# Graph tensor product on one Trainium2 core: the bf16 pieces of the edge features and a seventh one-hot row made by ScalarE

## The chip, the cores and the metric

The kernel runs on one core of a Trainium2 chip. The core has engines that run side by side, each through its own queue of instructions in a fixed order: TensorE (PE, matrix products; the profile shows its weight loads apart as PEld), VectorE (DVE, elementwise work), ScalarE (ACT, elementwise functions of one input), GpSimd (POOL, which issues the indirect transfers here) and SyncE (SP, which issues the plain ones). An engine that needs something from another waits for it, and what stands behind the waiting instruction in its queue waits too. The metric is the device time of one execution in microseconds. Lower is better.

## What is computed

```python
N, deg, C, L, DE = 10000, 64, 64, 1, 4
E = N * deg                                      # 640000 edges
M = (L + 1) ** 2                                 # 4
R = _silu(edge_feat @ w_rad)                     # (E, C)
xs = x[src]                                      # (E, C, M)
tp = jnp.einsum('eci,ef,ifo->eco', xs, Y, cg)    # (E, C, M)
msg = R[:, :, None] * tp
agg = _segment_sum(msg.reshape(-1, C * M), dst, N).reshape(N, C, M)
return jnp.einsum('ncm,cd->ndm', agg, w_mix)
```

Every edge fetches the 256 numbers of its source node, scales them by a small function of its four features, mixes them with its four numbers `Y`, and adds the result to its destination node. Source and destination are random.

## The kernel before

**Sorting.** The edges are cut into three parts (30, 35.5 and 34.5% of them). Each part is sorted by destination in two passes: `pass1` into 18 groups of 576 nodes, `pass2` of each group into up to 18 buckets of 32 nodes. A part and a group together are a segment. A pass works in chunks of 12 (first pass) or 11 (second) tiles of 128 edges. For a chunk, `spread` (lines 569 and 572, DVE) writes the edges' nine words into slots of rows (`X`), `rows` (lines 588 to 595) makes one one-hot matrix of 128 x 128 per tile (`oh`), which says to which row of the chunk an edge goes, `move` (lines 602 and 604, PE) multiplies the two, `evict` (line 609, ACT) copies the product out of PE's memory to `rt`, and `store` (line 613) has POOL scatter the rows to DRAM.

A one-hot is made in one of two ways. DVE compares (line 588): all its tiles in one instruction, 128 elements a tile. ACT squares the difference (line 594, one instruction of 128 elements per tile, into `sq`) and then takes relu(1 - 2 x square) of all its tiles in one (line 595). `ps.act`, 6 for both passes, is the number of tiles of a chunk that ACT does; DVE does the rest, so 6 of 12 or 5 of 11. Where a row of the chunk before is carried on, ACT squares one more (`tg`). `tables` computes where the rows of a pass go, in many small steps on all engines.

**Messages.** `messages` goes through units; a unit is one bucket of one part, with 5 tiles of 128 edges in the first part and 6 in the other two, 939 units in all. For a unit, `gather` (line 893, POOL) fetches the source rows with one indirect transfer per tile into one of seven buffers `xg`; `turn` (line 911, PE) turns the features, `turned` (line 916, ACT) copies them to `sT`, `radial` (lines 923 and 924, PE) multiplies with the weights, `silu` (line 927, ACT) applies the function; `spots` (lines 935 and 938, DVE) makes the destination one-hot times `Y`; `products` (line 945, DVE) scales `xg`; `sums` (line 958, PE) adds up the bucket; `evict` (lines 987 and 989) takes the sums out, and for the last part `mix` (line 1006) applies the output weights.

PE's `turn` is done in bf16 and the features are fp32, so each feature is split into three bf16 pieces that add up to it. `pieces` (lines 883 and 885, DVE) does this for a block of five buckets at once: cast the feature to bf16, written three times over (`e`); subtract the piece from the feature (`er`); cast the rest; subtract; cast. That is three casts and two subtractions a block, 210 blocks.

**Order.** In the first phase (up to some 500 us) only the first part is sorted. In the main phase the order of PE, DVE and ACT is the order in which the program text writes the instructions. `messages` is the outer loop: step k has four quarters, and in each quarter the listed functions are written for the unit k plus the given number (so `(silu, 1)` in step k is for unit k + 1). Between two quarters `groups` writes as many steps of the sorting of later parts and segments as are due. The order of POOL and SP is set by a scheduler from the dependences. `gather` stands five units ahead of `sums`.

Of the kernel before, what the change touches and what calls it, by code (L numbers as in the profile page):

```python
# [18 lines left out]
F = mybir.dt.float32  # L19
BF = mybir.dt.bfloat16  # L20
# [5 lines left out]
P = 128  # L26
B = 18
# [46 lines left out]
class Kernel:  # L74
# [276 lines left out]
    def tables(self, ps, D, nt, rows, kov, base, cap):  # L351
# [6 lines left out]
        assert N <= ps.NC <= 26 and nt >= T  # L358
        NC = ps.NC
        w = lambda nm, k, p=P, b=1, d=F: wk.tile([p, k], d, name=nm, tag=nm + ps.key, bufs=b)  # L360
# [12 lines left out]

        sums = w("sums", B * (T + 1))
        nc.vector.tensor_tensor_scan(sums[:H], ps.on, ps.cols, 0.0, op0=OP.mult, op1=OP.add)
# [39 lines left out]

        first, at = w("first", B), w("at", T * B)
        if ps.carry:
# [17 lines left out]
        eye = self.ident[:N, :N].unsqueeze(2).to_broadcast([N, N, J])  # L435
        bs, bd = w("bs", NC * J, NC, d=BF), w("bd", NC * J, NC)
        blk = lambda t: t[:N, :N * J].rearrange("p (c j) -> p c j", j=J)
# [74 lines left out]
    def route(self, ps, quad, nt, table):  # L512
# [65 lines left out]
        def rows(c):  # L578

            row, _ = MS[c // (2 * Q)]  # L580
            o = c % (2 * Q) * T
            m = min(T, nt - c * T)
            (_, _, _, tg), i = table(c)
            on = ps.carry and i > 0
            oh = self.ph.tile([P, 12, P], F, name="oh", bufs=3)
            v = max(m - ps.act, 0)
            if v:
                nc.vector.tensor_tensor(oh[:, :v, :], self.v128.unsqueeze(1).to_broadcast([P, v, P]),  # L588
                                        row[:, o:o + v].unsqueeze(2).to_broadcast([P, v, P]), op=OP.is_equal)

            at = [row[:, o + u:o + u + 1] for u in range(v, m)] + ([tg[:, i - 1:i]] if on else [])
            sq = self.ph.tile([P, 7, P], F, name="sq")
            for u, to in enumerate(at):
                nc.scalar.activation(sq[:, u, :], self.i128, AF.Square, bias=to, scale=-1.0)  # L594
            nc.scalar.activation(oh[:, v:v + len(at), :], sq[:, :len(at), :], AF.Relu, bias=self.ones[:, 0:1], scale=-2.0)  # L595
            XO[c] = (XO[c], oh, m, on)
# [235 lines left out]
    def messages(self):  # L832
# [4 lines left out]
        n = len(units)  # L837
        IDX, XG, PRE, ST_, RT, SS, VS, GP, GS, OLD, E9 = ({} for _ in range(11))

# [12 lines left out]
        def index(k):  # L852
# [16 lines left out]

        def pieces(k):  # L870

            g, j, s = units[k]
            if s or j % HB:
                return
            ut = sum(SPLIT[g[0]][1])
            a, z = j, min(j + HB, self.nb(g[1]))
            v = self.pay[g][:, a:z, :].rearrange("p b (t w) -> p (b t) w", w=W)[:, :, 5:9]
            n = (z - a) * ut
            E9[g, j // HB] = ph.tile([P, HB * MT, 3, 3, 4], BF, name="e9", bufs=2)
            r = ph.tile([P, HB * MT, 4], F, name="er", bufs=1)[:, :n]  # L880
            for q in range(3):
                e = E9[g, j // HB][:, :n, :, q, :]
                nc.vector.tensor_copy(e, (r if q else v).unsqueeze(2).to_broadcast([P, n, 3, 4]))
# [126 lines left out]
        def mixed(k, po):  # L1010
# [195 lines left out]
    def run(self):  # L1206
# [63 lines left out]
```

## Time and profile before

| | before |
|---|---|
| median of three runs | 8670.53 us (8667.58 to 8680.19) |
| span of the profiled execution, first to last instruction | 8660.7 us |
| what lies around the span, against the median | 9.8 us |
| busy: PE, DVE, POOL, ACT | 6942.9, 7173.7, 6041.3, 4089.0 us |
| gathers (line 893) | 5321 transfers, 5067.8 us of POOL |
| casts of `pieces` (line 883) | 630, of which 216 from 700 to 3300 us |

The profile has one execution. A row of a group of instructions gives its line, engine, operation, what it writes and reads, how often it ran, its busy time and the mean length of one, and behind a bar the idle time of the engine just before it and what ended that. A row of waits reads: engine, what waited, by what it was released, total us, how many times, the longest. The profiled execution's own time is not given apart from its span; the span is 6.9 us below the fastest of the three runs.

### The profile page before, as it was taken

What the parts mean: (1) busy time and instruction counts of PE and PEld (TensorE: products, weight loads), DVE (VectorE), ACT (ScalarE), POOL (GpSimd) and SP (SyncE); (2) the same over time, 40 slices, a digit from 0 to 9 for tenths busy, and PEclk for the clock granted to TensorE, in tenths of its full rate; (3) what the DMA queues carried; (4) which work ended last, traced back from release to release, by engine and by line L of the source; (5) the groups of instructions that cost most, each with busy time, mean ns of one, the idle gap of its engine ahead of it and who ended that gap; (6) DMA issues with size and microseconds to landing.
All of it is one profiled execution on the core that took longest, in us unless ns stands there. A gap on an engine that the chain in (4) does not pass through costs nothing. (4 is left out here: it accounts for less than half of the span.)

```text
span 8660.7 us, 149335 instructions
## 1 busy us (share of the span) xinstructions
PE 6942.9 (80%) x52148; PEld 6380.0 (74%) x52148; DVE 7173.7 (83%) x13741; ACT 4089.0 (47%) x11736; POOL 6041.3 (70%) x6308
## 2 busy tenths in 40 slices
PE   7978888888888778888888888866888878788875
PEld 6867777777777677777777777766777767777764
DVE  8989899889998788999989998877877768677754
ACT  6866555555556455454544554433333323333310
POOL 1236777667777767777777777777777777777775
PEclk9989999889999889999889899888998889888887
DMA  9313434334433434444444444444444444444442
GB/s 169 104 58 99 123 115 119 103 113 117 121 110 111 122 106 132 135 132 138 133 130 136 135 133 134 128 138 132 128 125 125 125 124 124 122 128 125 124 123 83
DMA packets 696289, 1056.64 MB, mean 122 GB/s; under 512 B 252018, under 2 KB 500226, under 8 KB 695536
## 3 DMA queue, kind: packets, MB, share of 16 engines
q0 software_dynamic: 286560, 746.71, 30.3%
q1 hardware_dynamic: 406384, 292.76, 12.2%
q8 instruction: 412, 6.75, 0.3%
q10 hardware_dynamic: 2592, 7.63, 0.3%
q14 instruction: 341, 2.79, 0.1%
HBM read 856.08 MB, written 207.12 MB: 123 GB/s over the span
## 5 line engine op out<-in xcount | busy, mean ns | idle before, releaser
L893 POOL DMA_INDIRECT xg<-in_x_dram,sidx x5321 | 5067.8, 952 | 1739.3 <-issue 1386.5
L602 PE MATMUL pr<-X,oh 128*128 128x126 f32 (+1 forms) x21112 | 2765.2, 289 | 395.7 <-ACT rt L609 215.6
L958 PE MATMUL G<-S,xg 128*128 128x128 f32 x21284 | 2953.1, 302 | 98.1 <-DVE Gp L987 62.8
L602 PEld LDWEIGHTS pr<-X,oh 128*128 128x128 f32 x21112 | 2638.2, 201 | 477.8 <-ACT rt L609 264.2
L958 PEld LDWEIGHTS G<-S,xg 128*128 128x128 f32 x21284 | 2803.5, 215 | 139.3 <-DVE Gp L987 86.2
L945 DVE TENSOR_TENSOR xg<-xg,pre 128x1536 f32<-128x1536 f32 (+1 forms) x939 | 1556.8, 1658 | 710.5 <-DMA xg<-in_x_dram,sidx 586.4
L594 ACT ACTIVATE sq<-i,rowf 128x128 f32<-128x128 f32 x5605 | 1735.7, 393 | 13.9 <-DVE rowf L559 13.4
L572 DVE TENSOR_TENSOR X<-dv,Wt 128x1512 f32<-128x1512 f32 (+4 forms) x958 | 1588.4, 1658 | 149.0 <-PE pr L602 94.8
L927 ACT ACTIVATE pre<-pre 128x384 f32<-128x384 f32 (+1 forms) x939 | 430.8, 459 | 1694.7 <-PE pre L924 1204.7
L595 ACT ACTIVATE oh<-sq,ones 128x768 f32<-128x768 f32 (+3 forms) x958 | 932.1, 973 | 32.9 <-issue 5.5
L938 DVE TENSOR_TENSOR S<-dv,pay 128x768 f32<-128x768 f32 (+1 forms) x939 | 857.4, 913 | 48.0 <-PE G L958 2.8
L613 POOL DMA_INDIRECT grp<-rt,idx x417 | 415.5, 996 | 585.9 <-ACT rt L609 240.1
L588 DVE TENSOR_TENSOR oh<-dv,rowf 128x640 f32<-128x640 f32 (+2 forms) x922 | 792.2, 864 | 0.5
L613 POOL DMA_INDIRECT bkt<-rt,idx x541 | 543.2, 1004 | 221.7 <-issue 125.8
L911 PE MATMUL pre<-identb,e 128*108 128x128 bf16 x1878 | 277.3, 231 | 523.4 <-DVE xg L945 513.6
L911 PEld LDWEIGHTS <-e 128*108 128x108 bf16 x1878 | 219.9, 133 | 604.5 <-issue 515.2
L916 ACT ACTIVATE sT<-pre 108x256 bf16<-108x256 f32 x939 | 353.5, 376 | 631.1 <-PE pre L911 628.4
L1006 PE MATMUL po<-wf,Gs 128*128 128x256 f32 (+2 forms) x1392 | 382.3, 436 | 150.7 <-DVE Gs L987 150.5
L542 ACT ACTIVATE pc<-pp 128x432 f32<-128x432 f32 (+3 forms) x506 | 243.7, 482 | 524.1 <-DVE pos L551 407.3
L1006 PEld LDWEIGHTS po<-wf,Gs 128*128 128x128 f32 (+2 forms) x1392 | 277.5, 205 | 238.3 <-DVE Gs L987 166.8
L609 ACT ACTIVATE rt<-pr 128x135 f32<-128x135 f32 (+1 forms) x958 | 258.8, 273 | 269.4 <-DMA bkt<-rt,idx 181.4
L923 PE MATMUL pre<-wr,sT 108*128 108x192 bf16 x939 | 240.2, 256 | 142.2 <-ACT sT L916 141.8
(240 smaller groups left out, 5309.3 us busy)
## 6 DMA issues: line engine op xcount, KB each, us to landing
xg<-in_x_dram,sidx POOLq DMA_INDIRECT x5321
sums<-Gp SPq DMA_DIRECT2D x626, 128.0 KB
old<-sums SPq DMA_DIRECT2D x626, 128.0 KB
bkt<-z SPq DMA_DIRECT2D x24, 994.5 KB
pay<-bkt SPq DMA_DIRECT2D x34, 486.0 KB
ys<-in_Y_dram SPq DMA_DIRECT2D x104, 96.0 KB
es<-in_edge_feat_dram SPq DMA_DIRECT2D x104, 96.0 KB
out_dram<-ot SPq DMA_DIRECT2D x69, 128.0 KB
```

The source lines that it names most:

```text
L572: nc.vector.tensor_tensor(X[:, :m, :].rearrange("p t (s w) -> p t s w", w=W), msk.unsqueeze(3).to_broadcast([P, m, ps.r, W]), QD[c // Q][1 ...
L588: nc.vector.tensor_tensor(oh[:, :v, :], self.v128.unsqueeze(1).to_broadcast([P, v, P]), row[:, o:o + v].unsqueeze(2).to_broadcast([P, v, P ...
L594: nc.scalar.activation(sq[:, u, :], self.i128, AF.Square, bias=to, scale=-1.0)
L595: nc.scalar.activation(oh[:, v:v + len(at), :], sq[:, :len(at), :], AF.Relu, bias=self.ones[:, 0:1], scale=-2.0)
L602: nc.tensor.matmul(pr[:, :ps.rw], oh[:, u, :], X[:, u, :], start=(u == 0), stop=(not on and u == m - 1))
L613: st = nc.gpsimd.indirect_dma_start(out=ps.dst, out_offset=bass.IndirectOffsetOnAxis(ap=idx[:, i:i + 1], axis=0), in_=RT.pop(c), in_offset ...
L893: nc.gpsimd.indirect_dma_start(out=xg[:, t, :], out_offset=None, in_=self.x, in_offset=bass.IndirectOffsetOnAxis(ap=si[:, u:u + 1], axis=0))
L911: nc.tensor.matmul(pre[:KR, 256 + 128 * h:384 + 128 * h], e[:, 36 * t:36 * t + KR], self.identb, start=True, stop=True)
L938: nc.vector.tensor_tensor(S[:, :ut], self.eq[:, :ut].unsqueeze(3).to_broadcast([P, ut, NB, 4]), pb[:, :, 1:5].unsqueeze(2).to_broadcast([P ...
L945: nc.vector.tensor_tensor(V, V, R.unsqueeze(3).to_broadcast([P, ut, 64, 4]), op=OP.mult)
L958: nc.tensor.matmul(G[:, h].rearrange("p n f -> p (n f)"), V[:, t, 32 * h:32 * h + 32, :].rearrange("p c i -> p (c i)"), S[:, t].rearrange( ...
L1006: nc.tensor.matmul(po[:nn, :256], Gs[:, h, f].rearrange("p b n -> p (b n)")[:, :nn], self.wf[:, h, f, :], start=(h + f == 0), stop=(h + f ...
```

## The change

Four things are changed.

- `pieces` is cut up. `piece(0)`, `piece(1)` and `piece(2)` make the three casts, now on ACT, and `rest(0)` and `rest(1)` make the two subtractions, still on DVE. They are spread over three steps: `piece(0)` and `rest(0)` in the step five units ahead, `piece(1)` and `rest(1)` in the next, `piece(2)` in the one after; before, all five stood in one step, four units ahead.
- In the main phase `act` is 7 instead of 6 for both passes, so ACT makes seven one-hots of a chunk (or eight with a carried row) and DVE five of twelve or four of eleven. `sq` grows from seven to eight planes.
- In `tables`, `sums` and `to` share one buffer (`x0`), and `at` and `bd` another (`x1`), where each had its own.
- `didx` has one buffer instead of two.

```diff
-            sq = self.ph.tile([P, 7, P], F, name="sq")
+            sq = self.ph.tile([P, ps.act + 1, P], F, name="sq")
...
-        sums = w("sums", B * (T + 1))
+        sums = wk.tile([P, XW], F, name="sums", tag="x0" + ps.key, bufs=1)[:, :B * (T + 1)]
...
-        first, at = w("first", B), w("at", T * B)
+        first = w("first", B)
+        at = wk.tile([P, XW], F, name="at", tag="x1" + ps.key, bufs=1)[:, :T * B]
...
-        bs, bd = w("bs", NC * J, NC, d=BF), w("bd", NC * J, NC)
+        bs = w("bs", NC * J, NC, d=BF)
+        bd = wk.tile([P, XW], F, name="bd", tag="x1" + ps.key, bufs=1)
...
-            to, tg = w("to", NC * J), w("tg", NC, b=2)
+            to, tg = wk.tile([P, XW], F, name="to", tag="x0" + ps.key, bufs=1), w("tg", NC, b=2)
...
-            di = ph.tile([P, B, MT], I32, name="didx", bufs=2)
+            di = ph.tile([P, B, MT], I32, name="didx", bufs=1)
...
-        def pieces(k):
...
-            E9[g, j // HB] = ph.tile([P, HB * MT, 3, 3, 4], BF, name="e9", bufs=2)
-            r = ph.tile([P, HB * MT, 4], F, name="er", bufs=1)[:, :n]
-            for q in range(3):
-                e = E9[g, j // HB][:, :n, :, q, :]
-                nc.vector.tensor_copy(e, (r if q else v).unsqueeze(2).to_broadcast([P, n, 3, 4]))
-                if q < 2:
-                    nc.vector.tensor_tensor(r, r if q else v, e[:, :, 0, :], op=OP.subtract)
+        def piece(q):
+            def cast(k):
...
+                if q == 0:
+                    E9[key] = ph.tile([P, HB * MT, 3, 3, 4], BF, name="e9", bufs=2)
+                    ER[key] = ph.tile([P, HB * MT, 4], F, name="er", bufs=1)
+                r = ER[key][:, :n] if q else v
+                nc.scalar.activation(E9[key][:, :n, :, q, :], r.unsqueeze(2).to_broadcast([P, n, 3, 4]), AF.Copy)
...
+        def rest(q):
+            def subtract(k):
...
+                nc.vector.tensor_tensor(r, r if q else v, E9[key][:, :n, 0, q, :], op=OP.subtract)
...
-        quarters = (((index, LI), (gather, LG), (fetch, 2), (turn, 2), (sums, 0), (silu, 1)), ((turned, 2), (spots, 1)),
-                    ((products, 1), (evict, -1), (pieces, 4)), ((radial, 2), (full, -1)))
+        quarters = (((index, LI), (gather, LG), (fetch, 2), (turn, 2), (sums, 0), (silu, 1), (piece(0), 5), (piece(1), 4),
+                     (piece(2), 3)), ((turned, 2), (spots, 1)),
+                    ((products, 1), (evict, -1), (rest(0), 5), (rest(1), 4)), ((radial, 2), (full, -1)))
...
             self.p1.NC = 14
+            self.p1.act = self.p2.act = 7
```

What this does to the order of ACT is shown at one block of five buckets of the first part. `pre` is the output of `radial`, on which `silu` works in place; `e` are the pieces, `pay` the edges' words, `er` what is left of a feature; `pc` and `Gp` are other copies out of PE's memory. Before:

```order
L927 ACTIVATE pre<-pre 128x320
L542 ACTIVATE pc<-pp 128x396
L916 ACTIVATE sT<-pre 108x256
L989 ACTIVATE Gp<-G 128x256
L594 ACTIVATE sq<-i_77,rowf 128x128 x6
L595 ACTIVATE oh<-sq,ones 128x768
L927 ACTIVATE pre<-pre 128x320
L916 ACTIVATE sT<-pre 108x256
L609 ACTIVATE rt<-pr 128x126
```

And the same stretch of ACT's queue in the changed kernel, where line numbers are up to 20 higher:

```order
L945 ACTIVATE pre<-pre 128x320
L892 ACTIVATE e_11177<-pay 128x75x4
L544 ACTIVATE pc<-pp 128x396
L934 ACTIVATE sT<-pre 108x256
L1007 ACTIVATE Gp<-G 128x256
L596 ACTIVATE sq<-i_77,rowf 128x128 x7
L597 ACTIVATE oh<-sq,ones 128x896
L945 ACTIVATE pre<-pre 128x320
L892 ACTIVATE e_11177<-er 128x75x4
L934 ACTIVATE sT<-pre 108x256
L611 ACTIVATE rt<-pr 128x126
```

A piece now stands between a `silu` and the copies `sT` and `rt` in both steps shown (the third piece of the block follows in the next step), and each group of squares is seven instead of six, with a Relu of 896 elements instead of 768. The second and third piece read `er`, which DVE writes one step earlier.

DVE's queue at the same block. Before, the five instructions of the block stand together behind `products` (line 945):

```order
L935 TENSOR_TENSOR dv<-dv,dlc 128x160
L938 TENSOR_TENSOR S<-dv,pay 128x640
L945 TENSOR_TENSOR xg<-xg,pre 128x1280
L883 CAST e_11198<-pay 128x75x4
L885 TENSOR_TENSOR er<-pay,e_11198 128x100
L883 CAST e_11198<-er 128x75x4
L885 TENSOR_TENSOR er<-er,e_11198 128x100
L883 CAST e_11198<-er 128x75x4
L569 TENSOR_TENSOR dv<-dv,slot 128x168
L572 TENSOR_TENSOR X<-dv,Wt_9931 128x1512
L338 TENSOR_TENSOR D_11085<-dv,two 128x270
L588 TENSOR_TENSOR oh<-dv,rowf 128x768
```

In the changed kernel one subtraction stands behind each of two `products` (now line 963), and the one-hot of DVE (now line 590) has 640 elements instead of 768:

```order
L963 TENSOR_TENSOR xg<-xg,pre 128x1280
L902 TENSOR_TENSOR er<-pay,e_11177 128x100
L590 TENSOR_TENSOR oh<-dv,rowf 128x640
L553 TENSOR_REDUCE pos<-pc 128x22
L338 TENSOR_TENSOR D_11144<-dv,two 128x720
L953 TENSOR_TENSOR dv<-dv,dlc 128x160
L956 TENSOR_TENSOR S<-dv,pay 128x640
L963 TENSOR_TENSOR xg<-xg,pre 128x1280
L902 TENSOR_TENSOR er<-er,e_11177 128x100
L571 TENSOR_TENSOR dv<-dv,slot 128x168
L574 TENSOR_TENSOR X<-dv,Wt_9977 128x1512
```

The three casts are gone from DVE's queue, and each subtraction reads a piece that ACT wrote in an earlier quarter of the same step. In POOL's queue the gathers keep their order, and some of the stores of rows come a unit earlier or later among them.

More of the change, by code (lines that the diff above doesn't have):

```diff
@@ L358, in tables @@
         assert N <= ps.NC <= 26 and nt >= T
-        NC = ps.NC
+        NC, XW = ps.NC, max(ps.NC * J, B * (T + 1))
         w = lambda nm, k, p=P, b=1, d=F: wk.tile([p, k], d, name=nm, tag=nm + ps.key, bufs=b)
@@ L837, in messages @@
         n = len(units)
-        IDX, XG, PRE, ST_, RT, SS, VS, GP, GS, OLD, E9 = ({} for _ in range(11))
+        IDX, XG, PRE, ST_, RT, SS, VS, GP, GS, OLD, E9, ER = ({} for _ in range(12))
         def quad(k):
@@ L868, in index, with block @@
             IDX[g] = (si, dl)
-        def pieces(k):
+        def block(k):
             g, j, s = units[k]
             if s or j % HB:
-                return
-            ut = sum(SPLIT[g[0]][1])
+                return None
             a, z = j, min(j + HB, self.nb(g[1]))
             v = self.pay[g][:, a:z, :].rearrange("p b (t w) -> p (b t) w", w=W)[:, :, 5:9]
-            n = (z - a) * ut
-            E9[g, j // HB] = ph.tile([P, HB * MT, 3, 3, 4], BF, name="e9", bufs=2)
-            r = ph.tile([P, HB * MT, 4], F, name="er", bufs=1)[:, :n]
-            for q in range(3):
-                e = E9[g, j // HB][:, :n, :, q, :]
-                nc.vector.tensor_copy(e, (r if q else v).unsqueeze(2).to_broadcast([P, n, 3, 4]))
-                if q < 2:
-                    nc.vector.tensor_tensor(r, r if q else v, e[:, :, 0, :], op=OP.subtract)
+            return (g, j // HB), v, (z - a) * sum(SPLIT[g[0]][1])
+        def piece(q):
+            def cast(k):
+                at = block(k)
+                if at is None:
+                    return
+                key, v, n = at
+                if q == 0:
[3 more added lines that the diff above has]
+                nc.scalar.activation(E9[key][:, :n, :, q, :], r.unsqueeze(2).to_broadcast([P, n, 3, 4]), AF.Copy)
+            return cast
+        def rest(q):
+            def subtract(k):
+                at = block(k)
+                if at is None:
+                    return
+                key, v, n = at
+                r = ER[key][:, :n]
+                nc.vector.tensor_tensor(r, r if q else v, E9[key][:, :n, 0, q, :], op=OP.subtract)
+            return subtract
         def gather(k):
```

## Prediction

> **What bounds the kernel now.** I read the busy shares first, then cut the span into stages at the times at which the gathers (`xg<-in_x_dram`, line 893) speed up or stop, then asked in each stage who waits for whom.
>
> ```profile
> span 8660.7 us, 149335 instructions
> PE 6942.9 (80%) x52148; PEld 6380.0 (74%) x52148; DVE 7173.7 (83%) x13741; ACT 4089.0 (47%) x11736; POOL 6041.3 (70%) x6308
> ```
>
> VectorE (DVE) has the largest share and ScalarE (ACT) the smallest of the computing engines, which would make any move from DVE to ACT a gain. That average hides the bound. The next view is busy time in five stretches: start and end, length, then PE, PEld, DVE, ACT, POOL with instructions in brackets, then the granted clock and DMA.
>
> ```profile
> 0.00:700.00 700.00, 554.50 (x4075) 484.65 (x4075) 607.91 (x1457) 494.33 (x1485) 174.80 (x193) 0.91 0.46 107
> 700.00:3300.00 2600.00, 2110.87 (x16559) 1965.24 (x16560) 2323.44 (x4519) 1446.44 (x4226) 1852.31 (x1927) 0.91 0.40 114
> 3300.00:5800.00 2500.00, 2036.35 (x15782) 1898.40 (x15782) 2235.98 (x4141) 1222.31 (x3473) 1896.41 (x1975) 0.90 0.47 134
> 5800.00:8440.00 2640.00, 2112.36 (x15033) 1922.48 (x15033) 1916.35 (x3440) 906.29 (x2499) 2002.54 (x2092) 0.88 0.44 125
> ```
>
> I call the last three rows stages A, B and C: the messages of the first, second and third part of the edges. POOL looks 71 to 76% busy, but a POOL instruction does not follow the last one at once. The waits of POOL (total us, times, longest) in stage A:
>
> ```profile
> POOL xg L893 <- issue: 405.8, 1332, 0.3
> POOL xg L893 <- PE G L958: 87.2, 45, 7.7
> ...
> POOL xg L893 <- PE pre L924: 16.6, 17, 4.6
> ...
> POOL xg L893 <- PE pre L911: 13.1, 18, 4.1
> ```
>
> Each transfer pays 405.8 / 1332 = 0.30 us of issue, which nothing releases. So POOL's own time is busy time plus 0.30 us per instruction. Stage A: 1852.3 + 1927 x 0.30 = 2430 of 2600, which leaves 170 us of true waiting. Stage B: 1896.4 + 592.5 = 2489 of 2500. Stage C: 2002.5 + 627.6 = 2630 of 2640. In B and C POOL is full, and the end of the program moves only if its transfers become shorter. Only A, with 170 us, and the start before it can be shortened by other engines.
>
> In A the engine that sets the pace is DVE: 2323 of 2600 us busy, and the longest row of its waiting there is the first one below. In C it waits for the gathers instead (second row):
>
> ```profile
> DVE X L572 <- PE pr L602: 57.8, 26, 5.6
> ```
>
> ```profile
> DVE xg L945 <- DMA xg<-in_x_dram,sidx: 497.3, 132, 6.8
> ```
>
> Of POOL's 170 us in A, 87.2 + 16.6 + 13.1 = 117 us are gathers that wait until PE work frees a buffer, that is, until the pipeline has moved on. That 117 us is what a faster DVE can give back; the rest are mostly row stores that are late for their own reasons.
>
> **The change part by part.** *DVE loses the casts of `pieces` and 128 elements of each one-hot.* Busy time of line 883 in stages A, B and from 5800 us on, then of line 588 in stage A, then the two forms of line 588:
>
> ```profile
> 700.00:3300.00 2600.00, 92.02 (x216) 0.91 0.40 114
> 3300.00:5800.00 2500.00, 64.37 (x186) 0.90 0.47 134
> 5800.00:8661.00 2861.00, 75.56 (x225) 0.87 0.43 122
> ```
>
> ```profile
> 700.00:3300.00 2600.00, 274.39 (x324) 0.91 0.40 114
> ```
>
> ```profile
> L588 DVE TENSOR_TENSOR oh<-dv,rowf 128x640 f32<-128x640 f32 x487 | 397.1, 815 | 0.4
> L588 DVE TENSOR_TENSOR oh<-dv,rowf 128x768 f32<-128x768 f32 x416 | 393.9, 947 | 0.0
> ```
>
> In A the casts give back 92 us. A one-hot of 768 elements costs 947 - 815 = 132 ns more than one of 640, so 128 elements less are worth 324 x 0.132 = 43 us. DVE is relieved of 135 us in A. In B and C it is relieved too, but there it waits for POOL, so I count nothing; the cover is POOL's queue, and it stays.
>
> *ACT gains the casts, one more square per chunk and a longer Relu.*
>
> ```profile
> L594 ACT ACTIVATE sq<-i,rowf 128x128 f32<-128x128 f32 x5605 | 1735.7, 393 | 13.9 <-DVE rowf L559 13.4
> L595 ACT ACTIVATE oh<-sq,ones 128x896 f32<-128x896 f32 x451 | 470.0, 1042 | 15.0 <-PE pr L602 0.3
> L595 ACT ACTIVATE oh<-sq,ones 128x768 f32<-128x768 f32 x471 | 439.8, 934 | 16.7 <-issue 5.5
> ...
> L714 ACT ACTIVATE Wt<-ys 128x96 f32<-128x96 f32 x208 | 61.4, 295 | 4.5 <-DVE X L572 4.5
> ...
> L595 ACT ACTIVATE oh<-sq,ones 128x512 f32<-128x512 f32 x18 | 13.0, 722 | 0.6
> ```
>
> A square takes 1735.7 / 5605 = 0.310 us of ACT's time (neighbours overlap, hence the mean of 393 ns), and 128 elements more of Relu cost 1042 - 934 = 0.108 us: 324 x 0.418 = 135 us in A. No row shows ACT making a piece; a piece in A has 300 elements. Its bounds are the copy of 96 elements at 0.295 us and the Relu of 512 at 0.722 us; I take the straight line between them, 0.295 + 204/416 x 0.427 = 0.504 us, so 216 x 0.504 = 109 us (64 to 156 by the bounds). Together 244 us: ACT goes from 1446 to 1690 of 2600 us, 65%. By throughput it has room.
>
> The Trainium skill, page "ScalarE: Activation LUTs", section "What ACT_TABLE_LOAD costs", has 186 ns plus 0.833 ns per element for an ACTIVATE with immediate scale and bias; the estimate from it is 436 ns for 300 elements, and the 109 us would be 94. Its section "Rules for kernel authors" speaks against the change: simple elementwise work belongs on VectorE, which is faster per element. The rows agree on the unit price, but that rule prices one instruction and not the queue it stands in.
>
> *ACT's queue is where it costs.* A piece stands right behind a silu and ahead of `sT`, `rt` and the squares; the second and third also wait for DVE's subtraction one step earlier. Whoever stands behind them is late, and that is PE. What PE waits for on ACT in A:
>
> ```profile
> PE pr L602 <- ACT rt L609: 137.7, 87, 11.8
> ...
> PE prep L387 <- ACT tot L394: 19.0, 1, 19.0
> PE pre L923 <- ACT sT L916: 18.3, 18, 1.6
> PE G L958 <- ACT Gp L989: 17.8, 22, 10.2
> ```
>
> That is 193 us for 1446 us of ACT work, 0.133 us per us. I charge the 244 us at that rate: 33 us, all of it against DVE's 135, which leaves 102. The bounds of this charge are nothing (PE is 81% busy in A and can make it up) and the full 244 us.
>
> *What is late next is POOL.* After 102 us POOL would have 170 - 102 = 68 us of slack in 2500, and each late store in its queue holds up the gathers behind it. I take three quarters of 102, 76 us; the ends are 0 and the 117 us of buffer waits.
>
> *POOL's transfers beside a cast.* Stage C, two of a block's three casts with the gathers beside them, and then the first and the last of the gathers counted below:
>
> ```profile
> 8182.33 0.34 DVE L883 CAST e<-pay 128x360 bf16<-128x360 f32 x1
> 8182.37 1.12 POOL L893 DMA_INDIRECT xg<-in_x_dram,sidx  x1 [0.30 <-issue]
> ...
> 8183.72 0.35 DVE L883 CAST e<-er 128x360 bf16<-128x360 f32 x1
> 8183.79 1.10 POOL L893 DMA_INDIRECT xg<-in_x_dram,sidx  x1 [0.30 <-issue]
> ```
>
> ```profile
> 3321.15 0.95 POOL L893 DMA_INDIRECT xg<-in_x_dram,sidx  x1 [0.30 <-issue]
> ```
>
> ```profile
> 8433.01 1.03 POOL L893 DMA_INDIRECT xg<-in_x_dram,sidx  x1 [0.30 <-issue]
> ```
>
> In B and C 236 gathers overlap a cast by over 0.05 us, from the one at 3321.15 to the one at 8433.01; their mean is 0.996 us, against 0.951 us for the 3344 others. Without casts POOL's full queue shortens by 236 x 0.045 = 11 us, a gain even where POOL is the bound.
>
> *At nothing:* the shared buffers `x0` and `x1` and the single `didx` are written and read by DVE in its own order, except `bd`, which PE reads one table earlier; the order of DVE's, ACT's and PE's rows up to the first main-phase chunk is unchanged. In POOL's queue 40 stores come up to six gathers later, where they hold it less, and ten up to six gathers earlier, each by 6 x 1.25 = 7.5 us: up to 75 us against, if each waited for all of that; I take nothing, since a store waits for `rt`, which ACT makes some steps ahead, and the forty speak the other way. Before 700 us ACT is as loaded as DVE (494 and 608 of 700 us); nothing there, within 10 us.
>
> **Sum.** 76 + 11 = 87 us off. The span is 8660.7 and the median of the runs 8670.5; the 9.8 us between them I carry over: 8583.5, say 8584.
>
> **Rivals.** *Hidden.* DVE is relieved, but stage A goes on at the pace of PE and of late stores; POOL's 11 us stay: about 8660. For it: PE at 81% with 138 us of waits for `rt`; against it: DVE's own waits are shorter than PE's. *ACT becomes the pace of A, slower.* Every longer burst and every wait for DVE's subtraction reaches `rt`, PE stalls, `X` is not freed, DVE waits. If the full 244 us showed, A would be 244 - 135 = 109 us longer, 98 after POOL's 11: 8769. It decides from 135/244 = 55% of ACT's added time showing, against the 13% that PE's waits show now. *The casts hold POOL for their whole length.* Then B and C lose 64.4 + 75.6 = 140 us of POOL's time instead of 11: 8670.5 - 76 - 140 = 8454. The gathers beside the block's casts last 0.17 and 0.15 us longer than 0.95, not 0.34, and the one at 3321.15 not at all, so I give it little. The Trainium skill, page "SBUF — State Buffer", section "SBUF: two separate sides", states this lock: a VectorE copy in its two-port mode locks GpSimd out of writing DMA descriptors for the whole instruction. The trace agrees that there is a cost, 0.045 us a gather, and not on its size.
>
> **How the numbers follow.** The forecast, 40 to 136 us off (117 + 11 + 8), has a chance of 0.58; the lock 0.05; hidden 0.15, a third of it over 0.2% faster; slower through ACT 0.22, its middle near 8715. Runs of this kernel tell 0.2%, 17 us, from no change. So faster 0.68, same 0.09, slower 0.23. The likeliest case alone reaches from 8534 to 8630; for 8 in 10 the range takes in the hidden case and the lower half of the slower one: 8530 to 8705.
>
> **What would show it.** Right: POOL's waits on `PE G` in stage A fall from 87 to under 40 us, the 5-tile stage ends some 75 us earlier, gathers stay at 1.25 us apart after it, and C's waits of DVE for gathers grow. Wrong: `PE pr <- ACT rt` above 250 us in A, or ACT waiting for `er` of line 885 for more than a few tens of us; or a piece far over 0.5 us.

## The result and the profile after

The changed kernel takes 8628.74 us (median of five runs, 8626.08 to 8636.13) against 8675.29 us for the kernel before (five runs, the three given above among them): a ratio of 0.9950, 95% interval 0.9939 to 0.9960. It is 46 us faster; 87 were forecast. The direction held, the size is about half. Two executions of one kernel below, `room`, took 8857.82 and 18081.52 us at granted clocks of 0.752 and 0.36; they count as slow and are left out of every comparison.

The page of the changed kernel:

```profile
span 8634.0 us, 150016 instructions
...
PE 6890.9 (80%) x52148; PEld 6320.9 (73%) x52148; DVE 6821.4 (79%) x13093; ACT 4619.2 (54%) x13164; POOL 6034.7 (70%) x6308
```

The work moved as written: DVE lost 352 us of busy time, ACT gained 530. The profiled execution took 8636.13 us, the slowest of the five, 2.1 us more than its span. All executions whose span is on record lie about 2 us above it, so the profiled execution of the kernel before (span 8660.7 us) took some 8663 us, 12 less than the median. The two traces therefore show only 27 us of the 46, and what follows is about shares of it. Busy time in the stretches of the prediction, in the changed kernel (columns as there: PE, PEld, DVE, ACT, POOL):

```profile
0.00:700.00 700.00, 547.06 (x4043) 478.44 (x4043) 597.87 (x1444) 499.31 (x1495) 174.86 (x193) 0.91 0.49 107
700.00:3300.00 2600.00, 2120.61 (x16695) 1971.72 (x16696) 2205.28 (x4329) 1647.91 (x4796) 1872.57 (x1947) 0.92 0.41 116
3300.00:5800.00 2500.00, 2033.34 (x15864) 1894.38 (x15863) 2140.66 (x3963) 1406.81 (x3957) 1892.67 (x1973) 0.91 0.46 134
5800.00:8440.00 2640.00, 2082.50 (x14963) 1885.36 (x14961) 1801.65 (x3194) 1045.51 (x2865) 1999.87 (x2097) 0.90 0.44 126
```

By the prediction's own reckoning POOL's true waiting in A is 2600 - 1872.6 - 1947 x 0.30 = 143 us, where it was 170. It should have been 94. A window of fixed length holds more of the work in a faster kernel, so waits and busy times in it are not those of the same work. The stages can be cut more sharply at `products`, one per unit in order: the first, the 314th (where the second part of the edges begins) and the 939th, from DVE's timeline of the kernel before and of the changed one.

```profile
710.07 1.48 DVE L945 TENSOR_TENSOR xg<-xg,pre 128x1280 f32<-128x1280 f32 x1
...
3249.43 1.74 DVE L945 TENSOR_TENSOR xg<-xg,pre 128x1536 f32<-128x1536 f32 x1
...
8579.77 1.75 DVE L945 TENSOR_TENSOR xg<-xg,pre 128x1536 f32<-128x1536 f32 x1 [4.27 <-DMA xg<-in_x_dram,sidx]
```

```profile
716.14 1.48 DVE L963 TENSOR_TENSOR xg<-xg,pre 128x1280 f32<-128x1280 f32 x1
...
3221.60 1.74 DVE L963 TENSOR_TENSOR xg<-xg,pre 128x1536 f32<-128x1536 f32 x1
...
8552.60 1.75 DVE L963 TENSOR_TENSOR xg<-xg,pre 128x1536 f32<-128x1536 f32 x1 [4.34 <-DMA xg<-in_x_dram,sidx]
```

Cut so, stage A went from 2539 to 2505 us, 34 less. Stages B and C together went from 5330 to 5331. All of the gain is in A, as forecast, and it is 34 where 76 stood. The start came 6 us later; over the profiles below it lies anywhere from 689 to 714 us, so nothing is read from it.

What A waits for now, in the changed kernel: POOL, PE, then DVE (two rows) and ACT, each an answer for 700 to 3300 us.

```profile
POOL xg L911 <- PE G L976: 64.7, 36, 6.0
...
POOL bkt L615 <- ACT rt L611: 19.7, 9, 8.0
POOL xg L911 <- PE pre L942: 14.0, 17, 3.5
...
POOL xg L911 <- PE pre L929: 10.9, 15, 4.9
```

```profile
PE pr L604 <- ACT rt L611: 203.4, 101, 13.5
```

```profile
DVE X L574 <- PE pr L604: 106.9, 41, 8.5
DVE xg L963 <- ACT pre L945: 54.3, 35, 4.3
```

```profile
ACT sT L934 <- PE pre L929: 230.8, 92, 9.2
...
ACT e L892 <- DVE er L902: 25.4, 19, 2.5
```

And two rows of the kernel before, for the same stretch, that were not shown:

```profile
DVE xg L945 <- ACT pre L927: 13.1, 12, 2.5
```

```profile
ACT sT L916 <- PE pre L911: 284.3, 117, 11.1
```

PE's wait for `rt` rose from 138 to 203 us, DVE's wait for a free `X` from 58 to 107, and its wait for `silu` from 13 to 54. DVE was given 135 us and now spends 90 more in these two waits. Not all of that comes from ACT's added work: in the run without pieces below, where ACT gains nothing, the wait for `silu` is 33 us too. The wait for `X` stays where it was there (62 us).

```profile
DVE xg L949 <- ACT pre L931: 33.2, 25, 3.1
```

ACT's own wait for DVE's subtractions, which I had named as a sign of failure, is 25 us in A.

### The profile page after: what moved, and what is told of

Read it like the earlier page. It is cut to its first block, busy times and chain, and to the rows that moved or that the text cites. A ratio compares the mean times of both kernels' runs of the same rounds, so it can differ in the third digit from the quotient of the medians.

```text
span 8634.0 us, 150016 instructions
## 1 busy us (share of the span) xinstructions
PE 6890.9 (80%) x52148; PEld 6320.9 (73%) x52148; DVE 6821.4 (79%) x13093; ACT 4619.2 (54%) x13164; POOL 6034.7 (70%) x6308
## 5 line engine op out<-in xcount | busy, mean ns | idle before, releaser
L604 PE MATMUL pr<-X,oh 128*128 128x126 f32 (+1 forms) x21112 | 2803.6, 291 | 490.1 <-ACT rt L611 321.7
L976 PE MATMUL G<-S,xg 128*128 128x128 f32 x21284 | 2863.7, 296 | 139.0 <-DVE Gp L1005 98.5
L976 PEld LDWEIGHTS G<-S,xg 128*128 128x128 f32 x21284 | 2715.3, 209 | 178.3 <-DVE Gp L1005 120.0
L596 ACT ACTIVATE sq<-i,rowf 128x128 f32<-128x128 f32 x6403 | 1969.4, 393 | 21.7 <-DVE rowf L561 21.2
L597 ACT ACTIVATE oh<-sq,ones 128x1024 f32<-128x1024 f32 (+4 forms) x958 | 1017.6, 1062 | 27.4 <-ACT sq L596 0.3
L590 DVE TENSOR_TENSOR oh<-dv,rowf 128x512 f32<-128x512 f32 (+2 forms) x904 | 684.0, 761 | 0.5
```

Of the source, the lines that this page charges most:

```text
L604: nc.tensor.matmul(pr[:, :ps.rw], oh[:, u, :], X[:, u, :], start=(u == 0), stop=(not on and u == m - 1))
L976: nc.tensor.matmul(G[:, h].rearrange("p n f -> p (n f)"), V[:, t, 32 * h:32 * h + 32, :].rearrange("p c i -> p (c i)"), S[:, t].rearrange( ...
```

## Experiments

Three readings stood against each other. **Q:** ACT's added time stands in its queue ahead of `rt` and `silu`, and what stands behind is paid back by PE and DVE. **W:** ACT waits for the subtractions and is held there. **P:** POOL's late stores set the pace of A whatever DVE does. All times are medians beside runs of the kernel before on the same chip; up to "The place of a square" that is one chip, number 7.

**The pieces alone.** The changed kernel without the line that sets `act`:

```diff
-            self.p1.act = self.p2.act = 7
```

> The changed kernel with ACT making six one-hots of a chunk as before; only the pieces move. Theory Q (ACT's added work stands in its queue ahead of rt and silu, PE then waits for rt and DVE for X, so most of the relief is paid back in stage A; the seventh one-hot gives DVE only 43 us there for 135 us of ACT, the pieces 92 us for about 100): 55 to 75 us under the kernel before, so better than the changed kernel (46 under). Theory W (ACT waiting for DVE's subtractions is what costs, which this keeps): 10 to 30 under, worse than the changed kernel. Theory P (POOL's late stores limit stage A whatever DVE does): 40 to 50 under, as the changed kernel.

Measured: 8583.44 us against 8662.95, ratio 0.9905 (0.9890 to 0.9919): 80 us under the kernel before, better than both kernels. That is far from W and P and 5 us beyond the range of Q. Windows and waits in A (DVE, PE, ACT):

```profile
700.00:3300.00 2600.00, 2126.63 (x16912) 1979.51 (x16912) 2282.81 (x4398) 1543.25 (x4524) 1909.65 (x1980) 0.92 0.41 118
```

```profile
DVE X L574 <- PE pr L604: 56.3, 24, 8.1
```

```profile
PE pr L604 <- ACT rt L611: 152.8, 87, 13.9
```

```profile
ACT sT L934 <- PE pre L929: 227.4, 96, 11.2
```

POOL's true waiting is 2600 - 1909.7 - 594 = 96 us. DVE's wait for `X` is what it was before (58), and ACT is busy for 97 us more in the window (part of this is that the window holds more of the work), while its wait at `sT`, the copy that often stands right behind a piece, fell by 57 us.

**The seventh one-hot alone.** The changed kernel with `pieces` on DVE as before.

> The kernel before with the seventh one-hot on ACT in the main phase and the shared buffers; the pieces stay on DVE. Theory Q: between 15 under and 10 over the kernel before. Theory W: 30 to 45 under, since no wait for a subtraction is added. Theory P: 25 to 45 under.

Measured: 8692.63 us, ratio 1.0033 (1.0020 to 1.0046): 30 us slower than before. The two halves add up, 30 - 80 = -50, to the changed kernel's -46.

```profile
700.00:3300.00 2600.00, 2094.57 (x16388) 1951.12 (x16388) 2259.75 (x4455) 1560.35 (x4521) 1834.05 (x1907) 0.91 0.39 113
```

```profile
DVE X L574 <- PE pr L604: 95.8, 39, 6.0
```

```profile
PE pr L604 <- ACT rt L611: 173.6, 96, 5.7
```

```profile
ACT sT L918 <- PE pre L913: 279.2, 114, 10.7
```

ACT is busy for 114 us more here than before. Its wait at `sT` stays (279 against 284), and DVE's wait for `X` goes from 58 to 96. POOL's true waiting is 194 us, above the 170 of before. Theory Q expected between 15 under and 10 over; the loss is larger, but of the sign that only Q allowed, and W and P are far off.

**DVE relieved, ACT not charged.** The kernel before, with the pieces made once and reused; it leaves out the casts and subtractions of all blocks but the first, so the radial factors belong to other edges.

```diff
+            if E9:
+                E9[g, j // HB] = next(iter(E9.values()))
+                return
...
```

`e9` has one buffer here, set to zero once.

> The kernel before in which the pieces are made only for the first block and used for all others, so the radial factor is that of wrong edges: DVE loses 92 us of casts and some 36 us of subtractions in stage A, and ACT gains nothing. Theories Q and W: 95 to 130 us under the kernel before, with POOL's waiting in stage A down from 170 to 60 us or less. Theory P: no more than 50 under, POOL's waiting stays over 120 us.

Measured: 8565.43 us, ratio 0.9887 (0.9873 to 0.9902): 98 us under, as Q and W had it. POOL's true waiting is 2600 - 1920.0 - 598.8 = 81 us, between the 60 of Q and W and the 120 of P.

```profile
700.00:3300.00 2600.00, 2137.46 (x17134) 1988.96 (x17132) 2286.72 (x4312) 1491.02 (x4357) 1920.04 (x1996) 0.93 0.42 119
```

P is out by the time. Stage A, cut at `products`, is 2451 us, 89 less, for the prediction's 92 us of casts and 36 us of subtractions (line 885 of the kernel before, stage A):

```profile
700.00:3300.00 2600.00, 36.42 (x144) 0.91 0.40 114
```

So a microsecond of DVE's work is worth 0.69 us of stage A. This prices the rest:

| kernel | DVE relieved in A, worth at 0.69 | ACT's added work in A (216 x 0.42, 324 x 0.418) | stage A | so ACT's work cost |
|---|---|---|---|---|
| before | | | 2539 | |
| pieces alone | 92, 64 | 91 | 2474 (-66) | nothing (-2) |
| seventh alone | 43, 30 | 135 | 2562 (+23) | 53, 0.39 per us |
| changed | 135, 93 | 226 | 2505 (-34) | 59 |

This reckons from rows. Busy time between the cuts at `products` needs no reckoning; the kernel before, the pieces alone, the seventh one-hot alone, the changed kernel and the one without pieces:

```profile
710.07:3249.43 2539.36, 2065.43 (x16171) 1922.24 (x16171) 2269.45 (x4401) 1412.18 (x4130) 1814.56 (x1887) 0.91 0.40 115
706.40:3180.20 2473.80, 2030.40 (x16171) 1890.54 (x16171) 2178.59 (x4191) 1478.09 (x4340) 1820.30 (x1887) 0.92 0.41 118
711.27:3273.29 2562.02, 2068.49 (x16170) 1926.64 (x16169) 2228.82 (x4386) 1534.64 (x4448) 1815.94 (x1888) 0.91 0.40 114
716.14:3221.60 2505.46, 2050.26 (x16174) 1906.54 (x16173) 2133.30 (x4176) 1599.27 (x4659) 1816.13 (x1888) 0.92 0.41 116
711.04:3161.86 2450.82, 2016.82 (x16169) 1876.93 (x16169) 2155.49 (x4051) 1411.66 (x4130) 1815.90 (x1887) 0.93 0.42 119
```

DVE is 91, 41, 136 and 114 us less busy than before, ACT 66, 122, 187 and 0 more. By this count a microsecond of DVE is worth 89 / 114 = 0.78, and ACT's added work costs 5, 54 and 72 us: 0.08 us per us for the pieces, 0.44 for the seventh one-hot. The split between the two holds by either count. But the pieces add only about half as much to ACT's busy time as the seventh one-hot, so a part of the difference is size. Each cost is a remainder of single traces, and kernels that differ by the step of room alone are 9 or 10 us apart in stage A (2474 and 2465, 2505 and 2495), so "nothing" means less than some 10 us.

The shared buffers and the single `didx` are in both halves. The pieces alone carry them at no cost that shows, so they do not explain the loss of the seventh one-hot.

**A step more room for the pieces.** The changed kernel with the pieces earlier, so that ACT finds the subtraction done.

```diff
-        quarters = (((index, LI), (gather, LG), (fetch, 2), (turn, 2), (sums, 0), (silu, 1), (piece(0), 5), (piece(1), 4),
+        quarters = (((index, LI), (gather, LG), (fetch, 2), (turn, 2), (sums, 0), (silu, 1), (piece(0), 7), (piece(1), 5),
...
-                    ((products, 1), (evict, -1), (rest(0), 5), (rest(1), 4)), ((radial, 2), (full, -1)))
+                    ((products, 1), (evict, -1), (rest(0), 7), (rest(1), 5)), ((radial, 2), (full, -1)))
```

`e9` has three buffers for it, `er` two, and `row` one.

> The changed kernel with one more step between each subtraction and the piece made of it (pieces seven, five and three units ahead, subtractions seven and five, three buffers e9, two er, one row). Theory W: ACT's wait for er falls from 288 us to under 60, and the time by 25 to 40 us below the changed kernel. Theory Q: the wait falls, the time stays within 10 us of the changed kernel. Theory P: the same as Q.

Measured: 8610.58 us, ratio 0.9938 (0.9924 to 0.9953): 52 under the kernel before, where the changed kernel is 46 under. No row of ACT waiting for `er` is left, and neither the ratio nor DVE's wait for `X` tells this from the changed kernel (107 us there; first row below). W is out: the 288 us that ACT waits for `er` over the span of the changed kernel (second row) cost nothing that shows.

```profile
DVE X L574 <- PE pr L604: 100.4, 39, 7.9
```

```profile
ACT e L892 <- DVE er L902: 288.3, 113, 17.2
```

**A square for nothing.** The kernel before with one more square per chunk in the main phase, behind the Relu, read by nobody; DVE is not relieved.

```diff
+            if not self.early:
+                more = self.ph.tile([P, P], F, name="more", bufs=1)
+                nc.scalar.activation(more, self.i128, AF.Square, bias=at[0], scale=-1.0)
```

> The kernel before with one more square on ACT for every chunk of the main phase that nobody reads, again, where the kernel before takes about 8665 us. Theory Q (ACT's own time ahead of rt and silu is paid back by PE and DVE at about 0.45 us per us of ACT): 35 to 55 us over the kernel before. Rival S (ACT has a third of stage A free, so its time costs 0.13 us per us, and the 30 us of the seventh one-hot come from something else): 5 to 18 over.

Measured: 8689.84 us against 8654.80, ratio 1.0042 (1.0028 to 1.0055): 35 us slower, the lower end of Q's 35 to 55 and not S's 5 to 18. Stage A is 2564 us, 25 longer, for 324 x 0.310 = 100 us of ACT.

```profile
700.00:3300.00 2600.00, 2101.28 (x16405) 1956.91 (x16406) 2296.81 (x4440) 1526.85 (x4522) 1836.88 (x1911) 0.91 0.39 113
```

```profile
DVE X L572 <- PE pr L605: 75.7, 32, 6.1
```

The square delays no one-hot of its own chunk. It only makes ACT later for what stands behind, and DVE's wait for `X` rises from 58 to 76.

**Five one-hots on ACT, with the pieces.**

```diff
-            self.p1.act = self.p2.act = 7
+            self.p1.act = self.p2.act = 5
```

> The pieces and five one-hots of a chunk on ACT, again, where the kernel before takes about 8665 us. Theory Q: 60 to 100 us under it, near the 80 of six one-hots with the pieces. Rival S: 35 to 55 under, since DVE pays its 43 us of stage A in full.

Measured: 8566.25 us, ratio 0.9899 (0.9884 to 0.9914): 89 us under, as Q had it, and not told apart from six with the pieces (0.9905, 0.9890 to 0.9919). In the second row the stage is cut at `products`.

```profile
700.00:3300.00 2600.00, 2140.47 (x17016) 1994.04 (x17016) 2337.07 (x4413) 1423.55 (x4210) 1916.11 (x1993) 0.92 0.41 119
701.00:3164.42 2463.42, 2027.85 (x16167) 1889.78 (x16167) 2218.70 (x4192) 1357.65 (x4021) 1815.04 (x1887) 0.92 0.41 118
```

In the fixed window DVE looks as busy as before the change (2337 against 2323), but that window holds more of the work. Between the cuts DVE is 51 us less busy than before and ACT 55 less, and stage A takes 2463 us, 76 less. Against six one-hots with the pieces DVE has 40 us more and ACT 120 less, and stage A is 10 us shorter: with DVE's 40 at 0.69 (28 us), ACT's 120 were worth 38, about 0.3 us per us. That is a price of ACT's time without any idle square, between the other two.

**The burst in two.** The changed kernel with the squares of a chunk written in two groups, four and the rest, with a turn for the other work between them.

```diff
...
+                if u == 4 and not self.early:
+                    yield "third"
                 nc.scalar.activation(sq[:, u, :], self.i128, AF.Square, bias=to, scale=-1.0)
...
```

> The changed kernel with each chunk's burst of squares written in two pieces, again, where the kernel before takes about 8665 us. If the length of the burst in front of silu and rt costs: 60 to 85 us under the kernel before (the changed kernel is 46 under). If ACT's total time or a late oh costs: 35 to 50 under, or less.

Measured: 8607.55 us, ratio 0.9950 (0.9936 to 0.9963), the same as the changed kernel; DVE's wait for `X` in A stays high:

```profile
DVE X L574 <- PE pr L606: 92.4, 39, 9.4
```

So the length of a single burst is not what costs, as far as the bursts are split here (some stay whole in the trace, where no other work is due between them). Whether it is ACT's time in all or a one-hot that is ready later, this run does not tell; the square for nothing shows that the first is enough for a part.

**Six and room.** The pieces alone, with the step of room.

> Six one-hots and the pieces on ACT, with one more step between each subtraction and its piece, again, where the kernel before takes about 8665 us. If ACT's wait for er costs in stage A too: 85 to 100 us under the kernel before (without the room 80 under). If it is hidden: 72 to 84 under.

Measured: 8571.65 us, ratio 0.9903 (0.9888 to 0.9918), the same as without the room: the wait for `er` is hidden here too.

**The place of a square.** A piece costs nothing that shows and a square 0.25 to 0.39 us per us. Is it the place? The kernel before with one idle square per unit right behind `silu`, where the pieces stand, or one right ahead of each `rt` of the main phase. These four runs and six further ones took place on three other chips (6, 10 and 8), where the kernel before takes a fifth longer (10592, 10609 and 10449 us), so each is compared only with the kernel before beside it.

```diff
             nc.scalar.activation(RT[k], RT[k], AF.Silu)
+            more = self.ph.tile([P, P], F, name="more", bufs=1)
+            nc.scalar.activation(more, self.i128, AF.Square, bias=self.ones[:, 0:1], scale=-1.0)
```

> The kernel before with one idle square of 128 elements on ACT in every unit, right behind silu, where the pieces stand in the changed kernel: 939 squares, against 833 in the kernel with one more square per chunk, which was 35 us over the kernel before. If the place counts (ACT waits for PE at the copy sT behind it, and the square fills that wait): 0 to 15 us over the kernel before, and ACT's wait at sT in stage A falls from 284 us by 40 or more. If ACT's time counts wherever it stands: 30 to 45 over.

> The kernel before with the same idle square right ahead of every copy rt of the main phase, 833 of them. If the place counts: 35 to 70 us over the kernel before, PE's wait for rt in stage A at 165 us or more (138 before). If only ACT's total time counts: 30 to 45 over.

> The kernel before with one idle square on ACT in every unit, right behind silu, again, where the kernel before takes about 8660 us. If the place counts: 0 to 15 us over the kernel before, and ACT's wait at sT in stage A falls from 284 us by 40 or more. If ACT's time counts wherever it stands: 30 to 45 over.

> The kernel before with the same idle square right ahead of every copy rt of the main phase, again, where the kernel before takes about 8660 us. If the place counts: 35 to 70 us over the kernel before, PE's wait for rt in stage A at 165 us or more (138 before). If only ACT's total time counts: 30 to 45 over.

| | chip 10 | chip 8 | per square |
|---|---|---|---|
| behind silu, 939 squares | 1.0023 (1.0015 to 1.0032), 21 us | 1.0019 (1.0008 to 1.0030), 17 us | 0.020 us |
| ahead of rt, 834 squares | 1.0046 (1.0034 to 1.0058), 49 us | 1.0040 (1.0025 to 1.0055), 47 us | 0.058 us |

The same square costs nearly three times as much ahead of `rt` as behind `silu`. Behind `silu` it costs 21 and 17 us, between the two expectations (0 to 15 if the place counts, 30 to 45 if it does not), so the place matters there and is not all. That it explains the difference where the kernel takes 8660 us is not shown, since these two runs were not had there. What the traces show there is the wait at `sT`: 284 us before, 227 with the pieces, 279 with the seventh one-hot. It is no clean measure of room either: with the pieces and the step of room it is 251, at the same time. And the pieces do not all stand in the better place: in stage A of the changed kernel 87 of the 210 are followed by an `sT` and 60 by an `rt`.

**Further runs on the slower chips.** The profile of the square behind `silu` (chip 8) shows another bound: waits of PE at its two big groups of products for nothing that the profile names, and of POOL for buffers, over the span.

```profile
PE G L960 <- issue: 458.4, 598, 7.2
PE pr L602 <- issue: 401.1, 537, 11.0
```

```profile
POOL xg L893 <- PE G L960: 657.5, 207, 10.8
```

POOL is no longer full: stages B and C together take 6537 us in it, against 5330. What the edits are worth there (the first four on chip 6, the last two on chip 10; their expectations were written for the kernel of 8660 us, and are not decided by these numbers):

> The kernel before with one more square on ACT for every chunk of the main phase, written to a scratch tile that nobody reads; it stands behind the Relu, and DVE is not relieved. About 100 us more of ACT in stage A. Theory Q (ACT's own time ahead of rt and silu is paid back by PE and DVE at about 0.45 us per us of ACT): 35 to 55 us over the kernel before. Rival S (ACT has a third of stage A free, so its time costs only what PE's waits showed, 0.13 us per us; the 30 us of the seventh one-hot come from something else): 5 to 18 over.

Measured there: 1.0036 (1.0023 to 1.0049).

> The changed kernel with ACT making five one-hots of a chunk, so DVE gets one more (seven of twelve, six of eleven) and the pieces stay on ACT. Theory Q: within 20 us of six one-hots with the pieces on ACT (8583): what ACT gives back, 135 us in stage A, is worth 40 to 60, what DVE takes on, 43 us, costs 35 to 43. Rival S: 8610 to 8630, since DVE pays its 43 us in full and ACT's relief is worth little.

Measured there: 0.9939 (0.9926 to 0.9951).

> The changed kernel with each chunk's burst of squares written in two pieces, four and then the rest with the Relu, so that silu, sT, Gp and sometimes rt of other work come between; the work is the same. Theory Q, in the form that it is the length of the burst in front of others that costs: 15 to 40 us under the changed kernel. If it is ACT's total time, or a late oh, that costs: within 10 us of it, or slower.

Measured there: 1.0088 (1.0074 to 1.0101).

> Six one-hots on ACT and the pieces on ACT, with one more step between each subtraction and its piece. The room gained some 10 us beside the changed kernel: 8568 to 8580, so the best of the kernels so far with a right result. If ACT's wait for er (328 us in all, mostly in stages B and C) is hidden behind POOL: 8578 to 8590.

Measured there: 0.9998 (0.9989 to 1.0006).

> The pieces and four one-hots of a chunk on ACT; DVE makes eight of twelve or seven of eleven. Against five (89 under the kernel before) DVE takes on 43 us in stage A at 0.68 us per us, 29 us, and ACT gives back 135 us at 0.35 or less, since less of it is waited for. 55 to 90 us under the kernel before; the bound in stages B and C is POOL and hides the rest.

The same edit with `act` at 4. Measured there: 0.9928 (0.9916 to 0.9939).

> The pieces and six one-hots on ACT, again, beside four: 75 to 85 us under the kernel before, as it was (80).

Measured there: 0.9985 (0.9976 to 0.9994).

Where PE is late, relieving DVE of the pieces is worth next to nothing. Taking one-hots off ACT is worth something: five instead of six gains 0.6% on chip 6 (0.9939 against 0.9998 with the step of room), four instead of six the same 0.6% on chip 10, so the second one taken off shows no gain of its own. Splitting the bursts, which changed nothing on chip 7, comes with a loss there; the changed kernel itself was not run on these chips. Whether four one-hots are better than five where the kernel takes 8660 us was not tried.

## Why the prediction was right and wrong

- *The bound: right.* Only stage A moved, by 34 us in the trace; B and C stayed within 1 us of 5330 with DVE 210 us less busy in them. POOL's queue covers them. Of the signs named, `POOL xg <- PE G` in A fell, to 65 and not under 40; the 5-tile stage ended 28 us earlier, not 75; and DVE's wait for gathers in C grew from 497 to 536 us (row below, the changed kernel from 5800 to 8440 us). None of the signs of being wrong came: `PE pr <- ACT rt` is 203 and not above 250, ACT's wait for `er` 25 us, a piece 0.44 to 0.51 us. The failure stayed below the limits that were set for it.

```profile
DVE xg L963 <- DMA xg<-in_x_dram,sidx: 536.0, 136, 6.5
```

- *DVE's relief: right.* 135 us of stage A were reckoned and 136 measured. Its worth, 0.69 to 0.78 us per us by the run without pieces, is near the three quarters that were taken for another reason; that is luck.
- *A piece at 0.504 us: somewhat high.* Not every piece of A has 300 elements, as was said; the smaller blocks have 180. All 210 of stage A in the changed kernel, then the two forms of 300 elements:

```profile
716.14:3221.60 2505.46, 88.10 (x210) 0.92 0.41 116
```

```profile
L892 ACT ACTIVATE e<-er 128x300 bf16<-128x300 f32 x104 | 46.1, 443 | 21.4 <-DVE er L902 20.8 <-DVE k L666 0.5
...
L892 ACT ACTIVATE e<-pay 128x300 bf16<-128x300 f32 x52 | 23.6, 453 | 0.2 <-PE pre L929 0.2
```

  The rows' straight line gave 0.504; the estimate from the Trainium skill, page "ScalarE: Activation LUTs", section "What ACT_TABLE_LOAD costs", was 436 ns, and the trace agrees with it to 4%. On the same page of the Trainium skill, "Rules for kernel authors" names relu, max, min, add and mul as work for VectorE. Carried over to the casts, it would have left them on DVE and lost 80 us here, since DVE was the queue that A waited for. The unit price holds for the one-hot (0.132 us on DVE against 0.418 on ACT for 128 elements), but for the casts only from 3300 us on. A cast of the rest, on DVE in the kernel before up to 3300 us and behind it, and on ACT in the changed kernel:

```profile
L883 DVE CAST e<-er 128x300 bf16<-128x300 f32 x102 | 47.5, 466 | 3.5
L883 DVE CAST e<-er 128x360 bf16<-128x360 f32 x204 | 71.2, 349 | 7.1
...
L892 ACT ACTIVATE e<-er 128x360 bf16<-128x360 f32 x208 | 103.8, 499 | 247.2 <-DVE er L902 246.7
```

  With 300 elements ACT is no dearer (443 against 466 ns); with 360 it is (499 against 349). Why the longer cast is the shorter one on DVE is open.
- *The charge for ACT's queue, 33 us: this step failed.* I took one rate, 0.133 us per us, from all of PE's waits on ACT over all of ACT's work, and charged squares and pieces alike. Measured, the added work cost 59 us in A (72 by busy time): the seventh one-hot 53, 0.39 us per us, and the pieces nothing that shows. A rate from existing waits is an average over work that is waited for and work that is not, and neither edit stood at the average. The two halves priced apart give 93 - 53 = 40 us for A, or 43 by their traces; 34 were measured. Of the squares' 0.39, the square for nothing shows 0.25 for making ACT later alone; whether the rest is the one-hot that is ready later is open. That the pieces cost so much less is measured; that it comes from their place is shown in part only, and they also add less to ACT's busy time.
- *Three quarters of what is left: near in size by luck, taken in the wrong place.* It belongs to DVE's relief, before ACT's cost and not after it. Its reason, that late stores hold up the gathers, was not tested by itself; only theory P, in which they set the pace whatever DVE does, is out.
- *The 11 us of POOL beside the casts: the time did not move.* POOL's busy time from 3300 to 8440 us, in the kernel before and the changed one:

```profile
3300.00:8440.00 5140.00, 3898.95 (x4067) 0.89 0.45 129
```

```profile
3300.00:8440.00 5140.00, 3892.54 (x4069) 0.90 0.45 129
```

  With two transfers more it was 6 us less busy, so the shorter transfers are there (of the gathers counted for the term, the 3344 beside no cast have a mean of 0.950 us rather than 0.951; the 11 stand), but B and C took 5331 us against 5330: other waits of POOL took their place in this trace. All ten traces of kernels that take some 8600 us, cut the same way, are kinder to the term: B and C take 5330, 5337 and 5340 us in the three kernels with the casts on DVE, 5321 to 5333 in the six with the casts on ACT (mean 5327 against 5336), and 5318 without any pieces. A gain of some 9 us is likely, and one pair of traces does not show it.
- *Rivals.* "Hidden" is out by stage A, 34 us shorter here and 89 without the pieces. "The casts hold POOL for their whole length" (140 us in B and C) is out by the lengths of B and C. "ACT becomes the pace" was right on the mechanism, PE late through `rt`, `X` late through PE, and needed 55% of ACT's time to show; 59 of 226 us did, 26%. It decided within the change, not over it: of the two edits, one gains 80 us and the other loses 30.
- *The sum.* In the traces 34 us came from A and nothing from the 11; the start came 6 us later. The other 19 of the 46 are that the execution profiled before was faster than its median and the one after slower. So the 9.8 us carried over from span to median were mostly that, and not time around the span.

## What to carry to other kernels

Price each half of an edit by itself: two moves from the same busy engine to the same idle one were worth -80 and +30 us, and the sum hid it. What idle time an engine has says little; look at which instruction of its queue the idle time stands in front of, and try added work right ahead of that wait, not ahead of an output for which the next engine is already waiting (0.020 against 0.058 us a square where this was tried). The price of relief is best measured by leaving the work out (0.69 to 0.78 us per us here), before deciding where to move it. Compare busy times over the same work, not over the same window of time.

## What was not expected of the hardware

On three chips the kernel before took a fifth longer (10449 to 10609 us) than on the one of the other experiments (8655 to 8663), with POOL's transfers as short as there (951 ns a gather, 952 in the kernel before). The granted clock was 0.83 to 0.84, against 0.90, and one trace has 859 us of waits of PE at its two big groups that the profile puts down to nothing, where the trace of the kernel before has none. The order of the versions changed there: the pieces alone gained 0.15% instead of 0.95%. What makes those chips slower is open.

On DVE, a cast of 300 elements took 457 to 466 ns and one of 360 elements 349 to 363. Of the smaller blocks, those of 180 took 332 to 341 ns and those of 216 took 300 to 312. No run here tests why.
